# Turning C and a quarter of x on VectorE, and adding 12 readouts by f32 transfers, in a gated mix of a state-space layer and an FFN

## The chip, the core and the metric

One core of one Trainium2 chip runs the kernel. The metric is the device time of one execution in microseconds (us), the median of several runs. One execution of the kernel before was also recorded by the hardware profiler; the profile and its trace come from that one. TensorE (PE), VectorE (DVE), ScalarE (ACT) and GpSimd (POOL) each work through a fixed list of instructions in order; SyncE (SP), ScalarE and GpSimd issue transfers (DMAs), which 16 DMA engines carry out.

## What is computed

x has 2048 tokens of 448 features; everything is bf16 at the borders. Cut to what matters:

```python
dt = exp(log_dt); Lam = Lambda_re + 1j*Lambda_im          # 448 lanes
Lam_bar = exp(dt*Lam)
B_bar = ((Lam_bar - 1)/Lam)[:, None] * (B_re + 1j*B_im)
Bu = x @ B_bar.T                                          # (2048, 448) complex
h[t] = Lam_bar * h[t-1] + Bu[t]                           # recurrence over tokens
a = 2*real(h @ (C_re + 1j*C_im).T) + x*Dskip
b = silu(x @ w1) @ w2                                     # 448 -> 1792 -> 448
g = sigmoid(sum(x*gate_w))                                # per token
out = g*a + (1 - g)*b
```

## The kernel before

**Tiling.** The tokens go in four chunks (tc 0 to 3) of 512, and each chunk in four blocks (tb) of 128. The complex lanes fill seven slots of 128 partitions (NSLOT): slots 0 to 2 the real parts of lanes 0 to 383, slots 4 to 6 their imaginary parts, slot 3 the real and imaginary parts of the last 64 lanes.

**Stages of a chunk.** `x_transposes` turns x on TensorE (32 transposes of 64 by 64 for a chunk, L508) into `xT`, with PSUM copied out by ScalarE or VectorE (L516, L518); chunk 0 has its own (L478). `x_products` (L663) multiplies xT with w1 (F tiles, 14 of 128 columns) and with B (B tiles, 7), two tiles at a time on the two row halves of the array; a pair takes two of eight PSUM banks. `evict` empties them: F tiles through ScalarE's SiLU (L634) into `aT`, B tiles into `UG`, by VectorE for chunk 0 (L640) and by ScalarE for the others (L642). `lanes` does the recurrence on VectorE: products with cosines and sines (L704), seven scans (L736) into `Gf` in f32, a cast of these back into `UG` (by GpSimd's transfers, L390, for chunks 0 to 2; by ScalarE, L746, for chunk 3), and four more products into `H[tc]`. For chunk 0 the first products are 18 small operations (L712 to L725), for the others four large ones. `gates` makes g and 1 - g and puts g*x*Dskip into `Tb` (which is `xnat`). `ffn2` (G in the calls, L774) multiplies aT with w2 per token block; ScalarE scales the result by 1 - g into `fe` (L780), and a GpSimd transfer adds it to Tb (L782). `readout` (C in the calls, L795) multiplies H with the scaled weights `CP`; VectorE multiplies the result by g and adds Tb into `ot` (L798), and SP stores it (L801).

**C.** `load_C` brings C in eight transfers into `Cnat`, which shares the tile H2C with H[2]. `readout_weights(k)` turns a quarter of it on TensorE (16 transposes of 56 by 56, L814), ScalarE scales the two parts into `ct` (L822, L825), and VectorE combines them into CP (L827, L830). The calls cp(0) to cp(3) stand between the G's of chunk 0. CP must be whole before the first readout.

**Order.** TensorE executes in the order of the program. Every other operation carries a cost, a priority and, for transfers, a number of bytes; the planner (`Plan.order`) goes through them with these costs and fixes the order of each engine: what can start first goes first, ties by the lower priority number. A transfer ends in its reckoning at the end of its queue's pipe; SP's and GpSimd's queues have separate pipes:

```python
free[o.eng] = t + o.cost
q = "pool" if o.eng == "pool" else "hw"
pipe[q] = max(pipe.get(q, 0.0), t + 0.9) + o.bytes / self.RATE[q]
o.end = pipe[q] + 0.8
```

The engines then keep that order, with semaphore waits for the true dependencies.

**Order on TensorE (the calls at L867 to L883).** F(0), B(0) and B(1) with the fillers (parameters, B's transposes, x's chunk 1); cp and G(0 to 3); F(1), one F(2), B(2) with x's chunk 2; G(4 to 7); C(0 to 3); F(2), B(3), F(3) with x's chunk 3; C(4 to 7), G(8 to 11); C(8 to 11), G(12 to 15), C(12 to 15).

Of the kernel before, what the change touches and what calls it, by code (L numbers as in the profile page):

```python
# [24 lines left out]
NFILL = 2  # L25
XCOL = [0, 128, 256, 320]
# [250 lines left out]
def bass_gated_mix__ssm_conv_s5__dense_activation_silu__prompt_kernel(nc, A_x, A_Lambda_re, A_Lambda_im, A_B_re, A_B_im, A_C_re, A_C_im,  # L277
               A_log_dt, A_Dskip, B_x, B_w1, B_w2, gate_w, out):
    with ExitStack() as ctx:
# [9 lines left out]
        xT = sb("xT", [128, 4, S_TOK], BF16)  # L289
# [3 lines left out]
        CP = sb("CP", [128, NSLOT, D_MOD], BF16)  # L293
# [5 lines left out]
        H2C = sb("H2C", [128, 3840], BF16)  # L299
        H = [H2C[:, 0:3584].rearrange("p (s n) -> p s n", s=NSLOT) if k == 2 else sb(f"H{k}", [128, NSLOT, CH], BF16) for k in range(4)]  # L300
        Cnat = H2C[:, :].rearrange("p (b l) -> p b l", b=4)
        cnn = [f"H2_{s}" for s in range(7)] + ["H2_3i"]
# [91 lines left out]
        def load_w1(q, k, a, b):  # L394

            cols = slice(w1cuts[k], w1cuts[k + 1])
            src = B_w1[320:448, cols] if a == 3 else B_w1[128 * a:128 * b, cols].rearrange("(b p) f -> p b f", p=128)
            load(q, w1s[:, 3, cols] if a == 3 else w1s[:, a:b, cols], src, " ".join(f"w1_{k}_{i}" for i in range(a, b)),
                 256 * (b - a) * (cols.stop - cols.start))
# [3 lines left out]
        load_w1("sp", 0, 0, 2)  # L403
        load_w1("act", 0, 2, 3)
        load_w1("act", 0, 3, 4)
        for k in range(1, len(w1cuts) - 2):
            load_w1("sp", k, 0, 3)
            load_w1("sp", k, 3, 4)
        for k, v in enumerate((A_log_dt, A_Lambda_re, A_Lambda_im)):
            load("sp", prm[k:k + 1, 0:448], v.rearrange("(o n) -> o n", o=1), f"prm{k}", 896)  # L410
        Bnat = H[3][:, :, 0:D_MOD]
# [5 lines left out]
        load_w1("sp", len(w1cuts) - 2, 0, 3)  # L417
        load_w1("sp", len(w1cuts) - 2, 3, 4)
# [8 lines left out]
        def load_C():  # L427

            for h in range(2):
                rows = lambda a: a[224 * h:224 * h + 224, :].rearrange("(b p) l -> p b l", p=56)  # L430
                to = Cnat[64 * h:64 * h + 56]
                load("sp", to[:, :, 0:448], rows(A_C_re), f"Cn0{h} " + (" ".join(cnn) if h == 0 else ""), 224 * 896)
                load("sp", to[:, :, 576:960], rows(A_C_im[:, 0:384]), f"Cn1{h}", 224 * 768)
                load("sp", to[:, :, 448:512], rows(A_C_im[:, 384:448]), f"Cn2{h}", 224 * 300)
                load("sp", to[:, :, 512:576], rows(A_C_re[:, 384:448]), f"Cn3{h}", 224 * 300)

        load_xn(1)
# [30 lines left out]
        def x0_transposes(q0, part, who):  # L468
# [12 lines left out]
            for h in range(2):  # L481
                src = lambda h=h: bk(tk, h).bitcast(BF16)[:, 0:256].rearrange("p (q b n) -> p q b n", q=2, n=64)
                dst = xT[:, q0:q0 + 2, 256 * part:256 * part + 256].rearrange("p q (b h n) -> p q b h n", h=2, n=64)[:, :, :, h, :]
# [11 lines left out]
        xn_of = {tc: {q: [f"xT{tc}_{h}" for h in range(2)] for q in range(4)} for tc in range(1, NCH)}  # L495
        xn_of[0] = {q: [f"xT0_{q}{part}{h}" for part in range(2) for h in range(2)] for q in range(4)}

        def x_transposes(tc, who):
# [13 lines left out]
            for h in range(2):  # L512
                src = lambda h=h: bk(tk, h).bitcast(BF16).rearrange("p (q b n) -> p q b n", q=4, b=4)
                dst = xT[:, :, tc * CH:(tc + 1) * CH].rearrange("p q (b h n) -> p q b h n", h=2, n=64)[:, :, :, h, :]
                if who[h] == "d":
                    DVE(lambda e, src=src, dst=dst: e.tensor_copy(dst, src()), [tk], [f"xT{tc}_{h}"], 0.69, 2.2, "xTe")  # L516
                else:
                    ACT(lambda e, src=src, dst=dst: e.activation(dst, src(), AF.Copy), [tk], [f"xT{tc}_{h}"], act_cost(1024), 2.2, "xTe")  # L518

# [103 lines left out]
        def evict(pair, tk):  # L623

            kinds = [t[0] for t in pair]
            for k, n in ((0, 2),) if pair[0][:2] == pair[-1][:2] and len(pair) == 2 else ((0, 1), (1, 1))[:len(pair)]:
# [12 lines left out]
                if tc == 0:  # L639
# [7 lines left out]
        def x_products(tiles, fill={}, wait=()):  # L647
# [10 lines left out]
            def steps(k, h, a, z):  # L658
                def body(pe):
                    for n, cut in list(enumerate(part[h]))[a:z]:  # L660
                        for b, ((i, p0), tile) in enumerate(zip(cut, pairs[k])):
                            tc = tile[1]
                            r = pe.matmul(bk(toks[k], b), weights(tile, p0, p0 + 64, i), xT[p0:p0 + 64, i, tc * CH:(tc + 1) * CH],  # L663
# [42 lines left out]
        def lanes(tc):  # L706
# [5 lines left out]
            if tc == 0:  # L712
# [20 lines left out]
            for s in (3, 0, 4, 1, 5, 2, 6) if tc else (0, 4, 1, 5, 2, 6, 3):  # L733
# [52 lines left out]
        def readout(tb):  # L786
# [3 lines left out]
            for n, (a, b) in enumerate(cuts):  # L790
# [6 lines left out]
                PE(mm, [f"H{tc}_{s}" for s in range(7)] + [f"CP{s}" for s in range(NSLOT)], [tk], NSLOT * (0.0025 + (b - a) / 2400), f"C{tc}")  # L797
                DVE(lambda e, tk=tk, a=a, b=b: e.scalar_tensor_tensor(ot[tb % NOT][:, a:b], bk(tk)[:, 0:b - a], g[:, tb:tb + 1],  # L798
# [4 lines left out]

        def readout_weights(k):

            tk = Ps(2)

            def mm(pe):
                for j, c0 in ((0, 128 * k), (1, 448 if k == 3 else 576 + 128 * k)):
                    for b in range(4):  # L810
                        o = j * 224 + 56 * b
                        for h in range(2):
                            p = slice(64 * h, 64 * h + 56)
                            r = pe.transpose(bk(tk, h).bitcast(BF16)[:, o:o + 56], Cnat[p, b, c0:c0 + 128], ident[p, p])  # L814
                return r
            PE(mm, [f"Cn{n}{h}" for n in range(4) for h in range(2)] + cnn + ["ident"], [tk], 8 * 0.0285, "CT")
            both_banks = lambda j: bk2(tk).rearrange("p h n -> p (h n)").bitcast(BF16).rearrange("p (h n) -> p h n", h=2)[:, :, 224 * j:224 * j + 224]
            re = lambda: both_banks(0)
            im = lambda: both_banks(1)
            in_two = lambda a: a.rearrange("p (h n) -> p h n", h=2)  # L820
            c, cn = ct[k % 2], f"ct{k % 2}"
            ACT(lambda e: e.activation(in_two(c[:, 0, :]), im(), AF.Copy, scale=sc2[:, k:k + 1]), [tk, "sc2"], [cn + "a"], act_cost(448, 1), 3, "ct")  # L822
            both = [cn + "a"]
            if k < 3:
                ACT(lambda e: e.activation(in_two(c[:, 1, :]), re(), AF.Copy, scale=sc2[:, k:k + 1]), [tk, "sc2"], [cn + "b"], act_cost(448, 1), 3, "ct")  # L825
                both.append(cn + "b")
            DVE(lambda e: e.scalar_tensor_tensor(in_two(CP[:, k, :]), re(), sc1[:, k:k + 1], in_two(c[:, 0, :]), ALU.mult, ALU.add),  # L827
                [tk, "sc1"] + both, [f"CP{k}"], 0.68, 1, "CP")
            if k < 3:
                DVE(lambda e: e.scalar_tensor_tensor(in_two(CP[:, 4 + k, :]), im(), nsc1[:, k:k + 1], in_two(c[:, 1, :]), ALU.mult, ALU.add),  # L830
                    [tk, "sc1"] + both, [f"CP{4 + k}"], 0.68, 1, "CP")

        def gates(tc):
# [3 lines left out]
               xnn + ["gwb"] + (["Gf0"] if tc else []), ["xg"], 1792, 19, "xg")  # L837
            tt(xnat[:, b4, :], xnat[:, b4, :], dkb[:, None, :].to_broadcast([128, 4, D_MOD]), ALU.mult,
               xnn + ["dkb"] + (["Gf0"] if tc else []), [f"xd{tc}"] + xnn, 1792, 19, "xd")
# [21 lines left out]
        def C(*tbs):  # L861
# [6 lines left out]
                   {(1, 0): [parameters], (K - 2, 0): turn_b[:1], K - 2: turn_b[1:2], K - 1: turn_b[2:], 7: xt(1, "da") + [lambda: lanes(0)]}, [K - 2])  # L868
# [3 lines left out]
        for f in cp(0) + G(0, 1) + cp(1, 2) + G(2, 3) + cp(3):  # L872
            f()
        x_products(F(1) + F(2, 0, 1) + B(2), {2: xt(2, "aa")})
# [44 lines left out]
```

## Time and profile before

| | us |
|---|---|
| median of 3 runs | 141.78 (141.49 to 141.81) |
| the profiled execution | 141.25 |
| its span, first to last instruction | 139.5 |
| VectorE busy, last lane product of chunk 3 ends at | 122.0, 128.16 |
| ScalarE busy | 90.3 |
| GpSimd busy | 39.2 |
| TensorE from the first to the last matmul | 0.76 to 136.73 |
| first readout, last four readouts begin on TensorE | 67.94, 131.38 |
| last transfer issued by SP before the stores, first store | 22.95, 70.3 |

Times in the profile are us from the span's start. The granted TensorE clock was 0.998 of full speed. The page's slices show TensorE busy nine tenths or more in all but the first and the last of 40. The DMA engines are busy through the first 27 us (the loads), and again in bursts, above all where GpSimd's transfers cast the scans (43 to 52, 64 to 76, 89 to 92 us).

### The profile page before, as it was taken

How to read it: one execution, taken by the hardware profiler on the slowest of the kernel's cores; microseconds unless marked ns; L12 is line 12 of the kernel's file. 1: busy time of each engine (PE TensorE's matmuls, PEld its weight loads, DVE VectorE, ACT ScalarE, POOL GpSimd, SP SyncE). 2: the span in 40 equal slices, each digit the busy share in tenths (PEclk: the TensorE clock that was granted, in tenths of full speed). 3: DMA queues.
4: the chain of work that ended last, by engine and by line, in shares of the span. 5: the costliest groups of instructions: out<-in, count | busy, mean ns of one | idle time of the engine just before them, and what ended most of it. 6: DMA issues, size and time to landing. Idle time of an engine off the chain costs nothing.

```text
span 139.5 us, 3000 instructions
## 1 busy us (share of the span) xinstructions
PE 135.9 (97%) x1201; PEld 67.0 (48%) x1201; DVE 122.0 (87%) x179; ACT 90.3 (65%) x157; POOL 39.2 (28%) x72
## 2 busy tenths in 40 slices
PE   7999999999999999999999999999999999999992
PEld 2445454455544544455544544444455555555561
DVE  0319999999999999999999999999999999997053
ACT  3349768999989999823694887799931268312300
POOL 7134040100248440227733001824000314022220
PEclk9999999999999999999999999999999999999999
DMA  4998999510156770104976200674202322323242
GB/s 136 337 294 243 363 320 238 177 42 0 31 79 94 129 110 1 38 15 73 157 131 155 38 5 0 95 133 79 38 4 97 66 33 36 83 83 61 40 94 71
DMA packets 17956, 14.71 MB, mean 105 GB/s; under 512 B 2835, under 2 KB 17814, under 8 KB 17942
## 3 DMA queue, kind: packets, MB, share of 16 engines
q0 software_dynamic: 6064, 5.51, 24.8%
q1 hardware_dynamic: 11318, 8.65, 20.7%
q10 hardware_dynamic: 560, 0.36, 0.8%
q8 instruction: 9, 0.15, 0.4%
q14 instruction: 5, 0.04, 0.1%
HBM read 7.17 MB, written 1.84 MB: 65 GB/s over the span
## 4 chain that ended last, share of the span: by engine, by line
PE 97%; DVE 0%; issue 0%
PE ps L663 46%; PE ps L774 31%; PE ps L795 15%; PE ps L463 2%; PE ps L508 1%; PE ps L478 1%; PE ps L814 1%; PE ps L604 1%; DVE ot L798 0%; PE ps L675 0%; PE ps L464 0%; PE ps L536 0%
## 5 line engine op out<-in xcount | busy, mean ns | idle before, releaser
L663 PE MATMUL ps<-xT,w1s 64*128 64x512 bf16 x392 | 48.5, 378 | 0.0
L774 PE MATMUL ps<-w2s,aT 128*128 128x448 bf16 x224 | 43.2, 353 | 0.0
L634 ACT ACTIVATE aT<-ps 128x1024 bf16<-128x1024 f32 (+1 forms) x30 | 28.7, 969 | 8.5 <-PE ps L663 8.4
L774 PEld LDWEIGHTS ps<-w2s,aT 128*128 128x128 bf16 x224 | 21.7, 98 | 20.4 <-ACT xnat L849 0.4
L663 PEld LDWEIGHTS ps<-xT,w1s 64*128 64x128 bf16 x392 | 19.7, 94 | 22.3 <-DVE xT L486 0.7
L663 PE MATMUL ps<-xT,BT 64*128 64x512 bf16 x196 | 25.8, 376 | 0.0
L782 POOL DMA_DIRECT2D xnat<-fe x16 | 14.1, 900 | 37.9 <-ACT fe L780 37.2
L780 ACT ACTIVATE fe<-ps,g 128x448 bf16<-128x448 f32 x16 | 10.1, 632 | 21.1 <-PE ps L774 21.0
L390 POOL DMA_DIRECT2D UG<-Gf x27 | 14.7, 549 | 20.9 <-DVE Gf L736 20.4
L736 DVE TENSOR_TENSOR_SCAN Gf<-rc,gin,H 128x512 f32<-128x512 f32 x14 | 17.2, 1268 | 0.0
L795 PE MATMUL ps<-CP,H 128*128 128x448 bf16 (+2 forms) x98 | 16.4, 326 | 0.0
L663 PEld LDWEIGHTS ps<-xT,BT 64*128 64x128 bf16 x196 | 10.8, 94 | 11.1 <-DVE Gf L562 0.2
L798 DVE SCALAR_TENSOR_TENSOR ot<-ps,g,xnat 128x448 bf16<-128x448 f32 (+2 forms) x18 | 10.8, 622 | 6.0 <-issue 4.6
L390 POOL DMA_DIRECT2D UG<-UG x8 | 4.8, 597 | 29.2 <-ACT UG L642 17.4
L704 DVE TENSOR_TENSOR H<-UG,COS 128x3584 bf16<-128x3584 bf16 (+4 forms) x10 | 12.6, 1266 | 0.0
L795 PEld LDWEIGHTS ps<-CP,H 128*128 128x128 bf16 x98 | 8.9, 98 | 7.5 <-DVE k L752 0.4
L642 ACT ACTIVATE UG<-ps 128x1024 bf16<-128x1024 f32 (+1 forms) x12 | 10.7, 923 | 1.4 <-PE ps L663 1.4
L842 ACT ACTIVATE junk<-xg 128x448 bf16<-128x448 bf16 x16 | 9.2, 574 | 2.1 <-DVE xg L704 2.0
L849 ACT ACTIVATE xnat<-xnat,g 128x448 bf16<-128x448 bf16 x16 | 9.8, 671 | 0.2
L704 DVE TENSOR_TENSOR PI<-UG,SIN 128x512 bf16<-128x512 bf16 (+2 forms) x13 | 9.1, 722 | 0.0
L704 DVE TENSOR_TENSOR PO<-UG,SIN 128x1536 bf16<-128x1536 bf16 (+1 forms) x8 | 8.7, 1087 | 0.1
L736 DVE TENSOR_TENSOR_SCAN Gf<-rc,gin,H2C 128x512 f32<-128x512 f32 x7 | 8.5, 1265 | 0.0
(102 smaller groups left out, 126.5 us busy)
## 6 DMA issues: line engine op xcount, KB each, us to landing
UG<-Gf POOLq DMA_DIRECT2D x21, 128.0 KB, 2.5
xnat<-fe POOLq DMA_DIRECT2D x16, 112.0 KB, 2.6
out_dram<-ot SPq DMA_DIRECT2D x15, 112.0 KB, 1.7
w2s<-in_B_w_dram SPq DMA_DIRECT2D x1, 1568.0 KB, 11.8
xnat<-in_A_x_dram SPq DMA_DIRECT2D x3, 448.0 KB, 6.1
w1s<-in_B_w_dram SPq DMA_DIRECT2D x1, 576.0 KB, 6.2
UG<-UG POOLq DMA_DIRECT2D x8, 64.0 KB, 2.2
H2C<-in_A_C_re_dram SPq DMA_DIRECT2D x2, 196.0 KB
```

The costliest lines, as they stand in the source:

```text
L390: P.add(q, lambda e: e.dma_start(dst, src), list(after), name.split(), 0.6 if q == "pool" else 0.5, prio, sem(), nbytes, tag="ld " + name)
L634: ACT(lambda e, src=src, dst=dst: e.activation(dst, src(), AF.Silu), [tk, "tbl"], [f"aT{tc % 2}_{m}" for m in names], act_cost(512 * n), 2 ...
L642: ACT(lambda e, src=src, dst=dst: e.activation(dst, src(), AF.Copy), [tk], [f"{un}{m}" for m in names], act_cost(512 * n), 5, "U")
L663: r = pe.matmul(bk(toks[k], b), weights(tile, p0, p0 + 64, i), xT[p0:p0 + 64, i, tc * CH:(tc + 1) * CH], start=(h == 0 and n == 0), stop=( ...
L704: DVE(lambda e: e.tensor_tensor(o, a, b, op), r, w, dve_cost(n, 2), prio, tag)
L736: DVE(lambda e, s=s, b=b, init=init: e.tensor_tensor_scan(Gf[:, s, :], rc[:, b:b + 1].to_broadcast([128, CH]), A[:, s, :], init, ALU.mult, ...
L774: r = pe.matmul(bk(tk)[:, 0:D_MOD], aT[tc % 2][:, fb, o:o + 128], w2s[:, fb, :], start=(fb == 0), stop=(fb == NFB - 1))
L780: ACT(lambda e: e.activation(f[:, :], bk(tk)[:, 0:D_MOD], AF.Copy, scale=g1[:, tb:tb + 1]), [tk, f"g1_{tc}"], [fn], act_cost(448, 1), 7, "fe")
L782: P.add("pool", lambda e: e.dma_start(Tb[:, tb, :], f[:, :], accum_op=ALU.add), [fn, f"Tb{tb}"], [f"Tb{tb}"], 0.94, 2, sem(), 115000, tag= ...
L795: r = pe.matmul(bk(tk)[:, 0:b - a], H[tc][:, s, o:o + 128], CP[:, s, a:b], start=(s == 0), stop=(s == NSLOT - 1))
L798: DVE(lambda e, tk=tk, a=a, b=b: e.scalar_tensor_tensor(ot[tb % NOT][:, a:b], bk(tk)[:, 0:b - a], g[:, tb:tb + 1], Tb[:, tb, a:b], ALU.mul ...
L849: ACT(lambda e, tb=tb: e.activation(Tb[:, tb, :], xnat[:, tb, :], AF.Copy, scale=g[:, tb:tb + 1]), [f"xd{tc}", f"g_{tc}"], [f"Tb{tb}"], ac ...
```

## The change

- **C.** `load_C` brings it in six transfers, rows on 128 partitions, into H[2] (the last block's 64 missing rows are zeroed by GpSimd). `readout_columns` turns it on VectorE in 32 by 32 blocks, four instructions, into H[3], and sixteen SP transfers, one for each pair of 32-partition groups, carry the blocks to their places in CP (runs of 64 bytes). `readout_weights` then scales CP in place. TensorE's transposes of C are gone, and the cp calls come after G(0 to 3).
- **x's chunk 3.** `x_blocks(3)` does the same with x's last 512 tokens: four block turns on VectorE, sixteen transfers into xT. TensorE's transposes and ScalarE's two copies of that chunk are gone.
- **Readouts 0 to 11.** ScalarE scales the PSUM result by g into an f32 tile (`ct`), a GpSimd transfer adds it to Tb, and SP stores Tb. Readouts 12 to 15 stay as they were.
- **Smaller edits.** lanes(0) takes the four large products; gates(1) has priority 20.3 for 19 and CP 20.5 for 1; x's chunk 1 and the parameters' transposes come one step earlier on TensorE; w1 is loaded in pieces of two row blocks each, the second ones of the first two column ranges from ScalarE's queue; the parameter rows are loaded before w1's third range; xT and CP have other layouts.

```diff
+L0M = True
+XT1K = 6
+S0 = (0, 4, 1, 5, 2, 6, 3)
+XT1 = "da"
+XPRIO = {2: 15, 3: 20.5}
+XBLK = (3,)
+XBEH = {2: "PI_0", 3: "H0_0"}
+UDVE = (0, 1, 2, 3, 4, 5, 6)
+OUTA = tuple(range(12))
+PRMF = (0, 0)
+CPRIO = 15.5
+CPP = 20.5
+GPR = (19, 20.3, 19, 19)
+CBEH = "PI_0"
...
-        xT = sb("xT", [128, 4, S_TOK], BF16)
+        xT = sb("xT", [128, NCH, 4, CH], BF16)
-        CP = sb("CP", [128, NSLOT, D_MOD], BF16)
+        CP = sb("CP", [128, NSLOT, CH], BF16)
...
+            if b == 4:
+                src = bass.AP(B_w1.tensor, 128 * a * F_FF + cols.start, [[F_FF, 128], [(320 - 128 * a) * F_FF, 2], [1, n]])
...
+        for k in range(2):
+            load_w1("sp", k, 0, 2)
+            load_w1("act", k, 2, 4)
         for k, v in enumerate((A_log_dt, A_Lambda_re, A_Lambda_im)):
             load("sp", prm[k:k + 1, 0:448], v.rearrange("(o n) -> o n", o=1), f"prm{k}", 896)
+        load_w1("sp", 2, 0, 2)
+        load_w1("sp", 2, 2, 4)
...
+            n = 0
+            for b0, b1, p in ((0, 3, 128), (3, 4, 64)):
+                rows = lambda a: a[128 * b0:128 * b0 + p * (b1 - b0), :].rearrange("(b p) l -> p b l", p=p)
+                for dst, src in (((0, 448), rows(A_C_re)), ((512, 896), rows(A_C_im[:, 0:384])), ((448, 512), rows(A_C_im[:, 384:448]))):
+                    load("sp", Cnat[0:p, b0:b1, dst[0]:dst[1]], src, f"Cn{n}" + (" " + " ".join(cnn) if n == 0 else ""),
+                         p * (b1 - b0) * max(300, 2 * (dst[1] - dst[0])), None, ["Cnz"] * b0)
+                    n += 1
+        POOL(lambda e: e.memset(Cnat[:, 3, :], 0.0), [], ["Cnz"], 0.9, 5)
...
+        def x_blocks(tc):
+            X32 = (xT[:, 3, :, :] if tc == 2 else H[3][:, 0:4, :]).rearrange("p m (q b i) -> p m q b i", q=4, i=32)
+            names = [f"X32_{k}" if tc == 3 else f"XT32_{k}" for k in range(4)]
+            held = [f"H3_{s}" for s in range(7)] + ["H3_3i"] if tc == 3 else xn_of[3][0]
+            turned = [f"BT{s}_{h}" for s in range(7) for h in range(2)]
+            xs = xnat[:, 4 * tc:4 * tc + 4, :]
+            for k, (q0, q1, c, b0, b1) in enumerate(((0, 3, 0, 0, 2), (0, 3, 0, 2, 4), (3, 4, XCOL[3], 0, 2), (3, 4, XCOL[3], 2, 4))):
+                n = q1 - q0
+                src = xs[:, b0:b1, c:c + 128 * n].rearrange("p b (q m i) -> p b q m i", q=n, i=32)
+                dst = X32.rearrange("p m q b i -> p b q m i")[:, b0:b1, q0:q1, :, :]
+                DVE(lambda e, dst=dst, src=src: e.transpose(dst, src), [f"xn{tc}", XBEH[tc]] + turned, [names[k]], 0.15 + 256 * n / 960, XPRIO[tc], "xTd")
+            k = sem()
+            for g in range(4):
+                for m in range(4):
+                    to = xT[32 * m:32 * m + 32, tc, :, :].rearrange("p q (b g i) -> p (q b) g i", b=4, i=32)[:, :, g, :]
+                    P.add("sp", lambda e, to=to, g=g, m=m: e.dma_start(to, X32[32 * g:32 * g + 32, m, :, :, :].rearrange("p q b i -> p (q b) i")),
+                          names + held, [f"xT{tc}_{g}{m}"], 0.66, 400, k, 32768, tag="xTm")
...
-            if tc == 0:
+            if tc == 0 and not L0M:
...
+                if tb in OUTA:
+                    f, fn = ct[tb // 2 % 2][:, tb % 2, :], f"ct{tb // 2 % 2}{'ab'[tb % 2]}"
+                    ACT(lambda e, tk=tk, f=f: e.activation(f, bk(tk)[:, 0:D_MOD], AF.Copy, scale=g[:, tb:tb + 1]),
+                        [tk, f"g_{tc}"], [fn], act_cost(448, 1), 3, "out")
+                    P.add("pool", lambda e, f=f: e.dma_start(Tb[:, tb, :], f, accum_op=ALU.add), [fn, f"Tb{tb}"], [f"Tb{tb}"], 0.94, 2, sem(), 230000, tag="Tb+")
+                    P.add("sp", lambda e: e.dma_start(out2[t0:t0 + 128, :], Tb[:, tb, :]), [f"Tb{tb}"], [], 0.3, 1, outs[tb % NOT], 128 * 896, tag="st")
+                    continue
...
+        def readout_columns():
+            C32 = H[3][:, :, :].rearrange("p s n -> p (s n)").rearrange("p (m t b i) -> p m t b i", m=4, b=4, i=32)
+            names = [f"X32_{k}" for k in range(4)]
...
+            for b in range(4):
+                src = Cnat[:, b, :].rearrange("p (t m i) -> p t m i", m=4, i=32)
+                dst = C32.rearrange("p m t b i -> p b t m i")[:, b, :, :, :]
+                DVE(lambda e, dst=dst, src=src: e.transpose(dst, src), [f"Cn{n}" for n in range(6)] + ["Cnz", CBEH] + cnn + turned, [names[b]],
+                    0.15 + 896 / 960, CPRIO, "CTd")
+            k = sem()
+            for g in range(4):
+                for m in range(4):
+                    to = CP[32 * m:32 * m + 32, :, :].rearrange("p t (b g i) -> p (t b) g i", b=4, i=32)[:, :, g, :]
+                    P.add("sp", lambda e, to=to, g=g, m=m: e.dma_start(to, C32[32 * g:32 * g + 32, m, :, :, :].rearrange("p t b i -> p (t b) i")),
+                          names + held, [f"CT{g}{m}"], 0.66, 400, k, 57344, tag="CTm")
         def readout_weights(k):
-            tk = Ps(2)
-            def mm(pe):
...
-            PE(mm, [f"Cn{n}{h}" for n in range(4) for h in range(2)] + cnn + ["ident"], [tk], 8 * 0.0285, "CT")
...
+            re, im = CP[:, k, 0:D_MOD], CP[:, 4 + k, 0:D_MOD] if k < 3 else None
...
+                ACT(lambda e: e.activation(c[:, 0, :], im, AF.Copy, scale=sc2[:, k:k + 1]), ctn + ["sc2"], [cn + "a"], act_cost(448, 1), 3, "ct")
...
-                   {(1, 0): [parameters], (K - 2, 0): turn_b[:1], K - 2: turn_b[1:2], K - 1: turn_b[2:], 7: xt(1, "da") + [lambda: lanes(0)]}, [K - 2])
+                   {PRMF: [parameters], (K - 2, 0): turn_b[:1], K - 2: turn_b[1:2], K - 1: turn_b[2:], XT1K: xt(1, XT1), 8: [lambda: lanes(0)] + [lambda: x_blocks(2)] * (2 in XBLK) + [readout_columns]}, [K - 2])
...
-        for f in cp(0) + G(0, 1) + cp(1, 2) + G(2, 3) + cp(3):
+        for f in G(0, 1, 2, 3):
+            f()
+        for f in cp(0, 1, 2, 3):
             f()
+        if 3 in XBLK:
+            x_blocks(3)
...
-        x_products(F(2, 1) + B(3) + F(3), {1: xt(3, "aa"), 9: [lambda: gates(3), lambda: lanes(3)]})
+        x_products(F(2, 1) + B(3) + F(3), {1: xt(3, "aa") if 3 not in XBLK else [], 9: [lambda: gates(3), lambda: lanes(3)]})
```

## The prediction

> **What bounds the kernel now.** I read the page's busy line and the chain of waits first, then the timelines of VectorE and ScalarE, then the DMA view in short windows. The profiled execution took 141.25 us, its span is 139.5, and 1.75 lie around it; the median of the runs shown is 141.78. A gain found in the span is taken from that median.
>
> ```profile
> PE 135.9 (97%) x1201; PEld 67.0 (48%) x1201; DVE 122.0 (87%) x179; ACT 90.3 (65%) x157; POOL 39.2 (28%) x72
> PE 97%; DVE 0%; issue 0%
> ```
>
> TensorE carries the chain from 0.76 to 136.73 us. Only what it has to execute, and what makes it wait, moves the time. The chain in order of time (start, length, what) shows what the change touches:
>
> ```profile
> 28.31 0.21 PE ps L814 x16
> ...
> 33.92 0.52 PE ps L814 x32
> ...
> 39.84 0.31 PE ps L814 x16
> ...
> 67.94 5.30 PE ps L795 x28
> ...
> 77.23 0.47 PE ps L508 x32
> ...
> 131.38 5.35 PE ps L795 x42
> ```
>
> L814 turns C and the last L508 turns x's last 512 tokens. Each piece follows its predecessor without a gap. L795 at 67.94 is the first readout, which needs C turned and scaled (CP) and H0; L795 at 131.38 needs H3.
>
> VectorE is the second engine to watch. Its timeline (start, length, what) near the end:
>
> ```profile
> 124.07 2.09 DVE L704 TENSOR_TENSOR H<-UG,COS 128x2048 bf16<-128x2048 bf16 x2
> 126.07 2.09 DVE L704 TENSOR_TENSOR H<-H,PO 128x2048 bf16<-128x2048 bf16 x2
> 132.80 0.69 DVE L798 SCALAR_TENSOR_TENSOR ot<-ps,g,xnat 128x448 bf16<-128x448 f32 x1 [4.64 <-issue]
> ```
>
> From 11 us to 128.16 it shows no idle time, and H3 is ready only 3.2 us before the readout at 131.38 wants it. What is added to VectorE or makes it wait beyond that is paid in full.
>
> **What TensorE loses.** The 64 matmuls of L814 go: 0.21 + 0.52 + 0.31 = 1.04 us. The 32 of L508 for the last 512 tokens go: 0.47. Together 1.51 us of the chain. Nothing is added to TensorE; parameter transposes and x's second chunk only move up by one step. The parameters' rows now have one load of 512 KB fewer ahead of them in SP's queue, 1.5 us at the 340 GB/s of those microseconds, and TensorE asks for them 1.5 us earlier (14 matmuls of 0.108): nothing gained or lost; up to 1.45 lost if they don't land earlier, up to 0.37 (its one wait for w1) won by the joined w1 loads. I take 0.
>
> **VectorE's sum.** By the distance from start to start: 12 readouts of 0.59 leave (7.1). lanes(0)'s 18 products become four of 1.9, 0.9, 1.1 and 1.95 as in lanes(1): 5.9 for 6.85, 1.0 less. Added are four block turns of C (896 columns each) and four of x (two of 768, two of 256). The trace has no such operation. Low end: the bf16 copy BT, 768 columns in 0.47, makes 3.5 us of all; high end: the scan, 512 columns in 1.13, makes 12.4. I take the rate nearest to it, one element per cycle, as the cast of 512 columns in 0.60: C 4 x 1.0, x 2 x 0.87 + 2 x 0.33, together 6.4. CP's seven operations stay. Net -1.7 us (-4.6 to +4.3): VectorE ends at about 126.5, TensorE now asks for H3 at 131.38 - 1.51 = 129.87; slack 3.4 us. At the high end it would be 2.6 late.
>
> **ScalarE, POOL, SP.** ScalarE gets 12 readouts of about 0.55 and one more CP operation of 0.52, and loses two copies of 0.9: +5.3 us on 90.3. Idle time covers it (8.5 us between 58.8 and 67.5, 5.1 before 107.58). POOL gets 12 issues of about 0.86 (L782's row) and a small memset; it idles 100 us. SP issues 32 transfers at some 0.6 (C's and B's loads took 0.54 to 0.88): it idles from 22.95 to 70.3. The f32 sums land some 2.6 us later (row of xnat<-fe) and only a store waits for them.
>
> **The sixteen transfers of C** decide the sign. Each moves 32 partitions x 28 runs of 64 B: 14,336 packets, 896 per DMA engine; x's sixteen make 512 per engine. No row shows 64 B from SBUF to SBUF. Three windows bound a packet. Full rows of 128 B from HBM dominate 22 to 23 us:
>
> ```profile
> DMA packets 409, 0.18 MB, mean 184 GB/s; under 512 B 260, under 2 KB 400, under 8 KB 409
> q1 hardware_dynamic: 389, 0.15, 91.6%
> ```
>
> 0.916 x 16 us over 389 is 37.7 ns. Stores from SBUF, 896 B (135 to 137 us), then 256 B (138.4 to 139.4 us):
>
> ```profile
> q1 hardware_dynamic: 146, 0.12, 16.9%
> ```
>
> ```profile
> q1 hardware_dynamic: 144, 0.03, 15.0%
> ```
>
> 5.41 us over 146 is 37.0 ns; 2.4 over 144 is 16.7. The line through both gives 10.6 ns at 64 B. Low end: bytes alone at w2's 381 GB/s, 2.7 ns. High end: the HBM row, 37.7. I take 10.6, since source and queue are those of the stores: C 9.5 us, x 5.4 us of each engine (2.4 to 33.8 and 1.4 to 19.3).
>
> The Trainium skill ("DMA: Bandwidth & Descriptors", "Why small descriptors are slow (HBM only)") says that transfers within SBUF escape the penalty on short descriptors. If it holds, the stores' line is the right one and not the HBM row; no row here shows it within SBUF.
>
> Now the times. lanes(0) starts at 27.5; its first three products end at 31.4 (C's turn is tied to the third, PI_0), the four turns at 35.4; C had landed by 27.9. The carry then needs 9.5 us beside 5.2 us of POOL's transfers (DMA share times length of the windows from 36 to 46 us: 0.08 x 2, 0.63 x 2, 0.34 x 3, 0.87 x 2, 0.99 x 1) and 1.7 to land (the stores' row): 51.8. Eight ScalarE operations of 0.52 and CP's make it 56; the first readout asks at 66.9. Cover 11 us, gone at 21 ns a packet. x's turn follows H0 and C's carry, its sixteen land by about 73, its products start at 82.07 - 1.51 = 80.6. H0 no longer has CP in front and comes earlier (some 54 for 57.8).
>
> One order is fixed beforehand: the planner charges 0.66 a transfer and has C landed at 35.4 + 15 x 0.66 + 1.9 = 47.2. So ScalarE's ct operations stand where 47.2 is right, and 51.8 makes ScalarE wait 4.6 us there, with SiLU evictions queued behind. Eight PSUM banks are four pairs of 1.51; TensorE goes on for three, 4.5 us, and ScalarE then clears a pair in 0.91. That leaves 0.1 us to pay, and each further microsecond costs one.
>
> **Sum.** 141.25 - 1.51 + 0.1 = 139.84 in the profiled execution, 141.78 - 1.51 + 0.1 = 140.37 in the median: forecast 140.4. Its own range is 139.5 (with the w1 wait and some more) to 141.3.
>
> **Rivals.**
> 1. *ScalarE waits for C's carry (slower).* Place: the first ct operations, F(1)'s evictions behind them, then TensorE without banks. Decides beyond 51.7 us of landing. At 15 ns a packet: 13.4 + 5.5 + 1.7 after 35.4 is 56.0, wait 8.8, less 4.5: 4.3 lost, 140.3 + 4.3 = 144.6. For it: DMA shares of 0.87 to 0.99 from 43 to 47 us and the planner's lack of contention. Against: the 16.7 ns of the stores of 256 B is already near it, with four times the bytes. 0.21.
> 2. *Short packets are no cheaper.* If 64 B cost what the stores' line gives at 512 B (24.9 ns): 22.3 + 6 + 1.7, landing at 65.4, 13.7 us lost: 154. At the HBM row's 37.7 ns some 164. Against: 256 B took less than half of 896 B. 0.07. The Trainium skill ("DMA: Bandwidth & Descriptors", "Specifications") speaks for this one: it puts the least size for line rate at 512 B, below which the engine reads, modifies and writes. By that the result would be the 154 of this rival; the trace's falling price from 896 to 256 B does not agree.
> 3. *Block turns at the scan's rate.* H3 2.6 late: 140.3 + 2.6 = 142.9. 0.06.
> 4. *Given back.* ct (4.2 us) now falls between 39 and 56 us, where ScalarE already has SiLU 6.9, x's copies 1.85, U's 3.3, fe 1.2: 17.45 for 17.0 us; the gates' 5.1 ahead of U's would hold four pairs of banks when FFN's second half asks for one: 1 to 2 us, 141.3 to 142.3. 0.10.
>
> **How the numbers follow.** Forecast 0.56, the rivals 0.21, 0.07, 0.06 and 0.10. 0.3% (0.4 us) is about what tells a change from none. Faster: the forecast's 0.56. Same: rival 4, 0.10. Slower: rivals 1 to 3, 0.34. The range reaches from 139.5 to 145.0, which holds the forecast, rivals 3 and 4 and most of rival 1; what lies beyond is rival 2, the worse part of rival 1 and little below.
>
> **What would show it.** Right: no L814, two L508 groups; C's sixteen landing near 52 us with a packet near 10 ns; block turns of about 1.0 and 0.9 us; chain still TensorE at 97%; H3 before 129.9. Wrong: ScalarE or VectorE idle near 48 us behind the CT transfers, gaps in TensorE after 50 us, SP issues of well over 0.7 us each, or a last readout that waits for VectorE.

## The result and the profile after

The changed kernel takes 153.03 us in the median of six runs (150.71 to 154.08), the kernel before 141.87 in the same comparison (141.49 to 142.43). The ratio is 1.0675, 95% interval 1.0589 to 1.0760: slower, where faster was forecast. The ratio is taken from the runs in the fast state alone (150.71, 150.80 and 152.93 us for the changed kernel), so it lies below the ratio of the two medians; the profiled execution is one of the longer runs. The profiled execution of the changed kernel took 153.14 us, its span is 151.3 (before 139.5): 11.8 us have to be found.

The page of the changed kernel: busy times, the granted TensorE clock in 40 slices, and the shares of the chain by engine.

```profile
span 151.3 us, 2853 instructions
...
PE 138.6 (92%) x1105; PEld 67.7 (45%) x1105; DVE 120.9 (80%) x161; ACT 95.5 (63%) x168; POOL 50.0 (33%) x85
...
PEclk9999999999999995699999999869999999999999
...
PE 52%; DVE 17%; SPq 13%; DMA 10%; issue 4%; ACT 2%; POOL 0%; DVEq 0%; ACTq 0%
```

TensorE, 97% of the chain before, now has about half of it; SP's queue and the DMAs have 23%. TensorE has 96 instructions less, as intended, and yet is busy 2.7 us longer: the clock row shows two dips (5, 6 and 8, 6 tenths), and each matmul takes longer there. The timeline of TensorE in the changed kernel (start, length, what; in brackets the idle time before it and what ended it) has these gaps after the first microseconds:

```profile
8.55 2.55 PE L701 MATMUL ps<-xT,w1s 64*128 64x512 bf16 x22 [0.69 <-DMA w1s<-in_B_w_dram]
...
58.15 6.35 PE L701 MATMUL ps<-xT,BT 64*128 64x512 bf16 x34 [5.13 <-ACT aT L672]
...
97.59 1.89 PE L701 MATMUL ps<-xT,w1s 64*128 64x512 bf16 x8 [2.53 <-ACT UG L680]
```

The stretch that follows each of the two large gaps is itself slow: 34 matmuls in 6.35 us, where 0.108 each makes 3.67. Windows of the same trace (length, busy time of PE, PEld, DVE, ACT and POOL with counts, granted clock, DMA share, GB/s) show the clock go down to half after the first gap and stay there for nearly 7 us, from about 56.4 to 63.3:

```profile
54.00:56.00 2.00, 0.00 (x0) 0.00 (x0) 2.00 (x2) 0.00 (x0) 0.00 (x0) 1.00 0.71 85
56.00:58.00 2.00, 0.00 (x0) 0.00 (x0) 0.29 (x1) 1.48 (x3) 0.00 (x0) 0.61 0.02 2
58.00:60.00 2.00, 1.85 (x10) 0.73 (x12) 1.24 (x2) 2.00 (x4) 0.00 (x0) 0.50 0.00 0
60.00:62.00 2.00, 2.00 (x14) 0.63 (x10) 2.00 (x3) 2.00 (x5) 0.06 (x1) 0.50 0.00 0
62.00:64.00 2.00, 2.00 (x16) 0.81 (x14) 2.00 (x4) 1.22 (x4) 0.99 (x2) 0.69 0.27 66
```

The account of TensorE up to the last four readouts, which begin at 142.44 for 131.38 before: +0.47 in the first 28 us, where TensorE waits for w1, +5.13 and +2.68 (6.35 - 3.67) for the first gap and its slow stretch, +2.53 for the second gap and +1.58 for its stretch (97.59 to 110.49 takes 12.90 us, the same 104 matmuls before 11.32), -1.51 for the transposes that are gone. Together +10.88 of 11.06; some 0.2 is unassigned, and 0.7 more lies behind the last matmuls.

What stands behind the gaps is in the view of waits of the changed kernel (who waits for what: us in total, times, longest):

```profile
DVE PO L742 <- DMA UG<-Gf: 7.7, 3, 3.3
...
ACT ct L875 <- DMA CP<-H: 6.8, 1, 6.8
...
PE ps L701 <- ACT aT L672: 5.1, 1, 5.1
ACT UG L680 <- DVE H L742: 4.3, 1, 4.3
...
PE ps L701 <- ACT UG L680: 2.5, 1, 2.5
```

The first gap is one chain: TensorE lacks banks because ScalarE's SiLU (aT) doesn't run; ScalarE stands 6.8 us before its first `ct` because C's sixteen transfers (CP<-H) have not landed. ScalarE's timeline around it:

```profile
47.77 1.96 ACT L672 ACTIVATE aT<-ps 128x1024 bf16<-128x1024 f32 x2
56.52 0.67 ACT L875 ACTIVATE ct<-CP,scc 128x448 f32<-128x448 bf16 x1 [6.79 <-DMA CP<-H]
57.09 1.00 ACT L672 ACTIVATE aT<-ps 128x1024 bf16<-128x1024 f32 x1
```

The second gap is another: VectorE's products of lanes(1) wait for casts (UG<-Gf), lanes(1) ends late, ScalarE may not yet overwrite UG[1] with U of chunk 3, and TensorE stops. VectorE's timeline there:

```profile
91.73 0.96 DVE L742 TENSOR_TENSOR PO<-UG,SIN 128x1536 bf16<-128x1536 bf16 x1 [3.35 <-DMA UG<-Gf]
93.68 1.23 DVE L742 TENSOR_TENSOR PO<-UG,SIN 128x2048 bf16<-128x2048 bf16 x1 [0.98 <-DMA UG<-Gf]
```

VectorE also came late to lanes(1): before it, it had waited 3.3 us for the casts of lanes(0) and 4.3 us in all for `ct`. H3, the one that the prediction watched on VectorE, is ready at 137.97 for a readout at 142.44.

Why C lands at 56.5: the chain of waits of the changed kernel in order of time, with the time that each transfer's issue held SP's queue,

```profile
36.45 0.73 SPq L866
...
43.38 1.60 SPq L866
...
48.83 2.92 SPq L866
...
53.45 0.66 SPq L866
54.15 2.34 DMA CP<-H
```

and the DMA view of the changed kernel, queue by queue (packets, MB, share of 16 engines), from 44 to 48 us and from 52 to 56 us:

```profile
q0 software_dynamic: 554, 0.50, 82.6%
q1 hardware_dynamic: 1901, 0.12, 32.9%
```

```profile
q1 hardware_dynamic: 5092, 0.32, 71.8%
q0 software_dynamic: 29, 0.02, 3.2%
```

q0 is GpSimd's queue (the casts of lanes(0)), q1 SP's. While the casts have the engines, C moves 1901 packets in 4 us; alone it moves 5092. The shares of the two queues add up to 115% from 44 to 48 us, so some packet times overlap. An issue on SP takes 0.66 us behind the casts, at 53.45, and up to 2.92 beside them.

### The profile page after: what moved, and what is told of

It is laid out like the page before. It is cut to its first block, busy times and chain, and to the rows that moved or that the text cites. A ratio compares the mean times of both kernels' runs of the same rounds, so it can differ in the third digit from the quotient of the medians.

```text
span 151.3 us, 2853 instructions
## 1 busy us (share of the span) xinstructions
PE 138.6 (92%) x1105; PEld 67.7 (45%) x1105; DVE 120.9 (80%) x161; ACT 95.5 (63%) x168; POOL 50.0 (33%) x85
## 4 chain that ended last, share of the span: by engine, by line
PE 52%; DVE 17%; SPq 13%; DMA 10%; issue 4%; ACT 2%; POOL 0%; DVEq 0%; ACTq 0%
PE ps L812 21%; PE ps L701 17%; PE ps L833 13%; SPq L866 11%; DMA UG<-Gf 5%; DMA w1s<-in_B_w_dram 3%; DVE H L860 3%; DVE UG L678 3%; SPq L403 2%; DVE Gf L565 2%; DMA CP<-H 2%; DVE H L742 1%; ACT aT L672 1%; DVE PI L742 1%; DVE ot L843 1%
## 5 line engine op out<-in xcount | busy, mean ns | idle before, releaser
L701 PE MATMUL ps<-xT,BT 64*128 64x512 bf16 x196 | 29.2, 415 | 5.1 <-ACT aT L672 5.1
L701 PEld LDWEIGHTS ps<-xT,w1s 64*128 64x128 bf16 x392 | 20.3, 95 | 26.4 <-issue 3.2
L774 DVE TENSOR_TENSOR_SCAN Gf<-rc,gin,H 128x512 f32<-128x512 f32 x21 | 25.4, 1267 | 0.1
L403 POOL DMA_DIRECT2D UG<-Gf x27 | 18.3, 776 | 11.8 <-DVE Gf L774 11.4
L833 PE MATMUL ps<-CP,H 128*128 128x448 bf16 (+2 forms) x126 | 21.9, 332 | 0.0
L701 PEld LDWEIGHTS ps<-xT,BT 64*128 64x128 bf16 x196 | 12.1, 102 | 18.3 <-ACT aT L672 5.9
L742 DVE TENSOR_TENSOR H<-UG,COS 128x3584 bf16<-128x3584 bf16 (+2 forms) x9 | 16.2, 1809 | 0.0
L833 PEld LDWEIGHTS ps<-CP,H 128*128 128x128 bf16 x126 | 11.6, 98 | 10.0 <-issue 0.4
L680 ACT ACTIVATE UG<-ps 128x1024 bf16<-128x1024 f32 (+1 forms) x12 | 10.6, 917 | 6.5 <-DVE H L742 4.3
L840 POOL DMA_DIRECT2D xnat<-ct x12 | 12.2, 1152 | 4.3 <-ACT ct L838 2.7
L843 DVE SCALAR_TENSOR_TENSOR ot<-ps,g,xnat 128x448 bf16<-128x448 f32 (+2 forms) x6 | 3.0, 525 | 7.2 <-PE ps L833 7.2
L742 DVE TENSOR_TENSOR PI<-UG,SIN 128x1536 bf16<-128x1536 bf16 (+1 forms) x8 | 8.5, 1078 | 0.0
```

What stands on the lines that cost most here:

```text
L403: P.add(q, lambda e: e.dma_start(dst, src), list(after), name.split(), 0.6 if q == "pool" else 0.5, prio, sem(), nbytes, tag="ld " + name)
L742: DVE(lambda e: e.tensor_tensor(o, a, b, op), r, w, dve_cost(n, 2), prio, tag)
L774: DVE(lambda e, s=s, b=b, init=init: e.tensor_tensor_scan(Gf[:, s, :], rc[:, b:b + 1].to_broadcast([128, CH]), A[:, s, :], init, ALU.mult, ...
L833: r = pe.matmul(bk(tk)[:, 0:b - a], H[tc][:, s, o:o + 128], CP[:, s, a:b], start=(s == 0), stop=(s == NSLOT - 1))
L840: P.add("pool", lambda e, f=f: e.dma_start(Tb[:, tb, :], f, accum_op=ALU.add), [fn, f"Tb{tb}"], [f"Tb{tb}"], 0.94, 2, sem(), 230000, tag=" ...
```

## Experiments

Times in brackets are the range of the runs; the kernel before took 141.5 to 141.9 in these comparisons.

**C reckoned late.** The planner reckoned that C lands at 47.8 (the prediction had estimated 47.2). Here it is told more bytes, so that it expects C at 58.5 and puts ScalarE's ct there.

```diff
-  names + held, [f"CT{g}{m}"], 0.66, 400, k, 57344, tag="CTm")
+  names + held, [f"CT{g}{m}"], 0.66, 400, k, 390000, tag="CTm")
```

> The planner is told that the sixteen transfers of C take as long as they did (landing near 58 us in its reckoning, for 47.8), so ct and CP stand later in ScalarE's and VectorE's order; nothing else changes. Theory A (ScalarE waits at ct for C's carry, and SiLU evictions queue behind it): ScalarE's 6.8 us of idle time before ct and TensorE's 5.1 us gap at 53 us go, and the half clock after it; C still lands near 56 us. VectorE's lanes(1) stays late, so the second gap (97 us) stays or grows: 143 to 148 us. Rival B (the f32 readouts through GpSimd's queue cost the time): no change, 151 to 153 us. Rival C (VectorE simply has too much to do before lanes(1), whoever waits): the first gap goes but all of it comes back in the second, 150 to 153 us.

Measured 153.93 us (153.22 to 154.96), ratio 1.0872 [1.0816, 1.0928]. The first gap and ScalarE's 6.8 us of idle time are gone, so the chain C, ct, SiLU, banks is shown. But the time came back at once, though not at the second gap, where rival C had it. TensorE's waits in this kernel:

```profile
PE ps L701 <- DMA xT<-H: 7.6, 1, 7.6
PE ps L833 <- DVE CP L881: 2.8, 1, 2.8
```

CP is now ready after the first readout wants it, and x's sixteen transfers, in turn behind it and among lanes(1)'s casts, run from 70.2 to 91 us and arrive 7.6 us late. There was no room to wait for C where it was; and the second carry has the same fault as the first.

**C turned early.** The four turns of C are no longer tied to a product of lanes(0); they run as soon as C has landed.

```diff
-CBEH = "PI_0"
+CBEH = "Cnz"
```

> C's block turns no longer wait for the third product of lanes(0); they go as soon as C has landed, so the carry runs before lanes(0)'s casts instead of beside them. Theory A: C lands near 41 us with SP issuing one transfer in 0.66 us, no wait at ct, no wait of VectorE for the casts near 48 us; lanes(1)'s scans start near 69 us for 75; first gap gone, second at most 2 us: 141 to 144 us. Rival D (64-byte packets are the cost wherever they run): C lands 18 us after its first issue again and little is gained, 149 us or more. Rival C: 147 us or more.

Measured 150.97 us (150.31 to 152.02), ratio 1.0664 [1.0603, 1.0726]. The issues go from 28.95 to 41.4 and the last lands at 45.4, eleven us earlier, though not near 41 as expected: the sixteen issues alone hold SP for 12.5 us, most of them before the casts fill the engines, and the last packets meet the casts. And the planner now reckons with 40.0 and puts ct accordingly: ScalarE still waits 5.8 us for CP<-H, TensorE 3.9 for ScalarE. Starting earlier moves the expected time with it. What makes ScalarE wait is the difference between the landing and the one reckoned with: 5.4 us here and a wait of 5.8, 8.7 us in the changed kernel and a wait of 6.8.

**No f32 readouts.** All readouts by VectorE again.

```diff
-OUTA = tuple(range(12))
+OUTA = ()
```

> All 16 readouts go through VectorE as before; no f32 sums through GpSimd's queue. Theory A: first gap unchanged (C's carry is untouched); VectorE has 7 us more to do, 2.4 of them before lanes(1) is through: second gap the same or up to 3 us more, 151 to 156 us. Rival B (the f32 transfers stand in front of lanes(1)'s casts and fill the DMA engines): second gap gone, 146 to 149 us.

Measured 151.75 us (151.25 to 151.95), ratio 1.0701 [1.0658, 1.0743]. The first gap stays (5.4). The second shrinks from 2.5 to 0.4 us, and VectorE no longer waits for lanes(1)'s casts, so the f32 transfers among them had a part in it; in exchange VectorE is late at the end, and the last readouts wait 1.9 us for H3. No net gain.

**x's chunk 3 by TensorE.** The second carry is taken away.

```diff
-XBLK = (3,)
+XBLK = ()
```

> x's last 512 tokens are turned by TensorE again; C stays with VectorE. Theory A: first gap unchanged at 5 us; lanes(1) comes 2.5 us earlier for the missing block turns and its casts have no transfers of x beside them, so the second gap goes: 146 to 149 us, of which 0.5 us is TensorE's own transposes. Rival B: no change in the second gap, 151 to 154 us.

Measured 149.18 us (148.04 to 149.43), ratio 1.0515 [1.0464, 1.0566]. The first gap is unchanged at 5.0, the second gone, and VectorE's wait for lanes(1)'s casts has shrunk from 4.3 to 0.2 us. Either of these two runs takes away, or nearly so, the second gap: it needs both x's part of the change and the f32 transfers. That both stand in the way of lanes(1)'s casts fits the waits; this run also takes x's block turns, 2.7 us, off VectorE, and does not tell the two apart.

**Both carries early and reckoned as they are.** The turns of C and of x run as soon as their source is there (x's priority raised), and the planner is given bytes that make each carry as long as it was seen to be.

```diff
-CBEH = "PI_0"; XBEH = {2: "PI_0", 3: "H0_0"}; XPRIO = {2: 15, 3: 20.5}
+CBEH = "Cnz";  XBEH = {2: "PI_0", 3: "Cnz"};  XPRIO = {2: 15, 3: 15}
-  [f"CT{g}{m}"], 0.66, 400, k, 57344       [f"xT{tc}_{g}{m}"], 0.66, 400, k, 32768
+  [f"CT{g}{m}"], 0.66, 400, k, 290000      [f"xT{tc}_{g}{m}"], 0.66, 400, k, 230000
```

> Both carries out of the casts' way and out of the fixed order's error: C is turned as soon as it has landed, the planner reckons its landing near 45 us (as measured in the run with C turned early), and x's last tokens are turned right behind it (priority 15, no wait for H0), while VectorE waited for casts before; their carry is reckoned to end near 62 us. Theory A (DMA engines shared between carries and casts, in an order fixed for less): no gap of TensorE above 1 us after 10 us, lanes(1)'s scans start near 66 us, H3 before the last readouts; 140.5 to 143 us. Rival C (VectorE has too much before lanes(1)): the gap near 95 us stays at 2 us or more and the time at 145 us or more.

Measured 143.06 us (142.13 to 145.71), ratio 1.0096 [1.0060, 1.0132]. Of the 6.75 points above the kernel before, 5.8 are gone with every instruction of the change still there. The place of the carries and the reckoning cost them, not the work; the run changes both at once and does not say what each is worth. C's issues go from 28.81 to 42.3, x's from 49.32 to 60.8. One gap above 1 us is left, where none was expected. What TensorE still waits for after 8 us: 0.73 for w1 and

```profile
89.53 1.04 PE L701 MATMUL ps<-xT,w1s 64*128 64x512 bf16 x8 [2.06 <-ACT UG L680]
```

**w1's loads as before.** The kernel above, with w1's second column range on SP's queue again, the parameter rows behind the third, and the parameters' transposes one step later on TensorE.

```diff
-PRMF = (0, 0)
+PRMF = (1, 0)
...
-for k in range(2):
-    load_w1("sp", k, 0, 2); load_w1("act", k, 2, 4)
+load_w1("sp", 0, 0, 2); load_w1("act", 0, 2, 4)
+for k in (1, 2):
+    load_w1("sp", k, 0, 2); load_w1("sp", k, 2, 4)
...
-load_w1("sp", 2, 0, 2); load_w1("sp", 2, 2, 4)
```

> As the run before, with w1's third range again ahead of the parameter rows, its second range on SP alone and the parameters' transposes one step later, as in the kernel before. Theory E (w1's third range lands 0.7 us after TensorE wants it): TensorE's wait for w1 at 7.9 us goes, 0.5 us less than the run with both early. Rival: no difference beyond 0.2 us, as another wait takes its place.

Measured 142.86 us (142.63 to 143.56), ratio 1.0091 [1.0061, 1.0121]: no gain that can be told. The wait for w1 is gone, and 0.84 us of waiting for ScalarE (UG) came up at 56.98. A wait of 0.7 us near 8 us was not what bounded the rest.

**C loaded before w2.** The kernel above with `load_C()` ahead of w2's load. VectorE no longer waits for C.

> As the run with w1 back, with C loaded ahead of w2, so that VectorE doesn't wait for C (0.9 us in the run with C turned early) before its block turns. Theory A: C's carry starts where VectorE's order has it, some 28.5 us; within 0.5 us of the run with w1 back, 0 to 0.9 us better if VectorE's end decides. If w2 becomes late for the FFN's second half at 28 us, 1 us worse.

Measured 142.19 us (141.30 to 143.67), ratio 1.0029 [0.9997, 1.0062]: not to be told from the kernel before. One gap of 1.21 us is left, at 87.79, for UG of ScalarE behind lanes(1).

**C alone.** The kernel of 142.86 us (w1 as before, C early) with x's chunk 3 by TensorE.

```diff
-XBLK = (3,)
+XBLK = ()
```

> C turned early by VectorE and carried, with the honest reckoning; x's last tokens by TensorE, w1 as before, readouts 0 to 11 still by ScalarE and f32 transfers. Theory A: no second carry at all, lanes(1) some 2.5 us earlier than with x's block turns; TensorE saves 1.04 us only: 140.7 to 142 us. Rival B (f32 transfers cost): 143 us or more.

Measured 143.02 us (142.72 to 143.56), ratio 1.0107 [1.0071, 1.0143]. It was expected at 140.7 to 142. Three small waits of TensorE for ScalarE's SiLU, 0.25 to 0.59 us each, have taken the place of the one near 89. The time is the one that the rival gave, by which the f32 transfers cost it; the runs with fewer of them, below, are no faster. Against the same kernel with x's turn (142.86) there is no difference: rightly placed, x's turn neither wins nor costs anything that can be told.

**Four sevenths of C's bytes.** The changed kernel itself, each transfer of C with 16 runs of 64 B a partition for 28, the number of issues and the order the same. The last three slots of CP are set to zero by GpSimd (its line is left out here), so the outputs leave out part of the state.

```diff
-  to = CP[32 * m:32 * m + 32, :, :].rearrange("p t (b g i) -> p (t b) g i", b=4, i=32)[:, :, g, :]
+  to = CP[32 * m:32 * m + 32, :, :].rearrange("p t (b g i) -> p (t b) g i", b=4, i=32)[:, 0:16, g, :]
-  C32[32 * g:32 * g + 32, m, :, :, :].rearrange("p t b i -> p (t b) i")
+  C32[32 * g:32 * g + 32, m, 0:4, :, :].rearrange("p t b i -> p (t b) i")
```

> The changed kernel with four of seven slots carried: each of the sixteen transfers of C moves 16 runs of 64 B a partition and not 28; the last three slots of CP stay at zero (a POOL memset near 5 us), so the outputs leave out part of the state. Number of issues, their place and the planned order are unchanged. Theory A (the carry is late because the bytes of packets share the DMA engines with the casts of lanes(0), C's share 8.9 us of each engine): 3.8 us of it go, C lands near 52, ScalarE's wait for it falls from 6.8 to about 3, TensorE's gap from 5.1 to 1 to 1.7, the stretch at half clock behind it shortens or goes: 147 to 149.5. Rival B (the number of issues on SP, 16 of them at up to 2.9 us, or the casts alone set it): the gap stays at 5, 152 to 154.

Measured 147.42 us (146.81 to 148.37), ratio 1.0409 [1.0368, 1.0450]. Waits of this kernel (its lines are one higher):

```profile
ACT ct L876 <- DMA CP<-H: 3.3, 1, 3.3
```

```profile
PE ps L702 <- ACT UG L681: 3.8, 1, 3.8
PE ps L702 <- ACT aT L673: 1.7, 1, 1.7
```

ScalarE's wait falls by 3.5 us and the gap by 3.4, for 3.8 us of packets taken out (three sevenths of 8.9): here the packets decide, not the number of issues. The 34 matmuls behind the gap take 3.84 us now for 6.35; a gap of 1.7 us cost no clock. The second gap has grown to 3.8 us, and VectorE waits 4.2 us for lanes(1)'s casts as before.

**Fewer f32 readouts in the good order.** The kernel of 142.19 us with readouts 0 to 3 by VectorE, so that no f32 transfer stands among lanes(1)'s casts (the f32 readouts' stores get semaphores of their own); and the same with none at all.

```diff
-OUTA = tuple(range(12))
+OUTA = tuple(range(4, 12))
```

> The kernel with both turns early, w1 back and C loaded first (142.19), with readouts 0 to 3 by VectorE again and 4 to 11 through f32 transfers. Theory A (the last gap of 1.21 us in TensorE, U's eviction behind lanes(1), comes from four f32 transfers of readouts that stand among lanes(1)'s casts on POOL's queue between 69 and 77 us): the gap goes, VectorE gets 2.4 us more early where it waits anyhow, 140.4 to 141.4. Rival (it was x's carry and the casts' own length): gap stays near 1, 142 to 142.6.

> As the run before, with none of the readouts through f32 transfers (all by VectorE). VectorE then has 7.1 us more work than in 142.19. Theory A: the gap near 88 us goes as well, but lanes(3) ends late as it did when the same was done to the changed kernel (its readout waited 1.9 us there): 141 to 143. Rival (VectorE's relief by 12 readouts isn't needed once the turns are early, since the 6.4 us of turns now lie in idle time): under 141.

Measured 142.55 us (141.86 to 144.45), ratio 1.0055 [1.0034, 1.0076], and 144.36 (144.15 to 145.06), ratio 1.0193 [1.0166, 1.0219]. With readouts 0 to 3 by VectorE no cast is waited for, and the gap has not gone but grown:

```profile
88.66 1.04 PE L701 MATMUL ps<-xT,w1s 64*128 64x512 bf16 x8 [1.73 <-ACT UG L680]
```

VectorE shows no idle time from 11 to 95 us in this kernel. So the expectation fell, and what is left as the cause of the last gap is VectorE's own lateness. Its block turns come before lanes(1), and the readouts that leave it begin only at 68 us. With none of the f32 readouts the last readouts wait 1.9 us for H3 besides: the relief is needed at the end.

**The gates of chunk 2 later.** The kernel of 142.19 us; two VectorE products of 1.07 us go behind lanes(1)'s scans.

```diff
-GPR = (19, 20.3, 19, 19)
+GPR = (19, 20.3, 22, 19)
```

> The kernel of 142.19 us with the gates of the third chunk (two VectorE products of 1.07 us, at 71.8 and 74.0) behind lanes(1)'s scans and not between them. Theory C (what is left of the loss is the order on VectorE: the block turns come before lanes(1), the relief by f32 readouts only after it, so lanes(1) ends 1.2 us after TensorE needs UG[1] read; the run with readouts 0 to 3 on VectorE showed a gap of 1.73 us with no wait for a cast): lanes(1)'s scans end 2.1 us earlier, the gap near 88 us goes, median 140.8 to 141.4, under before's 141.6. Rival (the casts of lanes(1) between f32 transfers on POOL's queue set it): the wait of 1.4 us for a cast grows to 3 and the gap stays at 1: 142 to 142.5.

Measured 141.18 us (140.28 to 142.77), beside 141.90 (141.29 to 143.97) of the kernel before on the same chip: ratio 0.9953 [0.9923, 0.9982]. TensorE's waits in this kernel, all of 0.2 us and more:

```profile
PE ps L479 <- PEq L962: 0.8, 1, 0.8
PE ps L833 <- ACT aT L672: 0.2, 1, 0.2
```

The first of them is there in every run. The gap is gone, though VectorE's one wait for a cast grew from 1.4 to 2.4 us: the order on VectorE had set it. The last four readouts begin at 130.01, 1.37 us earlier than in the kernel before, nearly all of the 1.51 that the transposes were worth; the profiled execution took 140.28 us, its span is 138.5. This version holds the three main parts of the change, with w1's loads nearly as before; it is faster than the kernel before by about a half per cent.

## Why the prediction was wrong, point by point

**What TensorE loses: right.** The transposes are gone, 1.51 us. "I take 0" for w1 and the parameters was 0.47 off, inside the bounds it gave, though it was w1's third range that came late and not the parameter rows.

**VectorE's sum: right as a sum, blind to its order.** A block turn of C takes 1.0 us as predicted, those of x 0.97 and 0.44 for 0.87 and 0.33:

```profile
32.34 4.08 DVE L860 STREAM_TRANSPOSE H<-H 128x896 bf16<-128x896 bf16 x4
...
51.19 0.96 DVE L742 TENSOR_TENSOR PO<-UG,SIN 128x1536 bf16<-128x1536 bf16 x1 [3.34 <-DMA UG<-Gf]
...
58.76 0.69 DVE L881 SCALAR_TENSOR_TENSOR CP<-CP,sc1s,ct 128x448 bf16<-128x448 bf16 x1 [2.47 <-ACT ct L876]
```

Busy time went from 122.0 to 120.9 (net -1.1 for -1.7), and H3 has 4.5 us of slack. But the step checked VectorE at one place, the end. The turns are added before lanes(1), the relief comes after 68 us, and lanes(1) has a use of its own: UG[1] must be read before U of chunk 3 may be written. Even with everything else mended that cost 1.2 to 1.7 us at 88 us, until two products were put later.

**The sixteen transfers of C: the price right, the company wrong.** A 64-byte packet alone takes 0.718 x 64 us / 5092 = 9.0 ns, and 9.8 over the whole carry (10.6 taken). The step that failed is the "5.2 us of POOL's transfers" beside it. They were summed over 36 to 46 us, while the landing that this gave was at 51.8: the window ended before the carry did. The trace of before had the rest; its GpSimd queue from 44 to 48 us and from 48 to 52 us:

```profile
q0 software_dynamic: 661, 0.60, 92.8%
```

```profile
q0 software_dynamic: 502, 0.43, 74.6%
```

With the windows from 36 to 44 (35.5% and 43.6%) and the 1.1% after 52 that is 4 x (0.355 + 0.436 + 0.928 + 0.746 + 0.011) = 9.9 us, and 35.4 + 9.5 + 9.9 + 1.7 = 56.5, the time at which ScalarE got C. The changed kernel's own trace has much the same: the turns end at 36.45, and from there to 56.5 us C's packets hold 44.6% of the engines' time and the casts 47.9%, 8.9 and 9.6 us. The experiment with four sevenths of the bytes bears the sum out.

**The cover: the path right, the size by luck.** By the prediction's own rule a landing at 56.5 gives a wait of 9.3, less 4.5 of banks: 4.8 lost. TensorE lost 5.13, but both terms were too large. ScalarE waited 6.8 us, since the work that it had before ct lasted to 49.7; TensorE went on for 3.3 us of that, to 53.0, and began again 1.6 us after C was there: 6.8 - 3.3 + 1.6 = 5.1. So rival 1, ScalarE waiting for C's carry, is what happened, and three of the signs that were named for going wrong came: ScalarE idle from 49.7, a gap in TensorE after 50, issues on SP of up to 2.92 us. Its chance, 0.21, was too low because of the short window; its price, 144.6, left out what a gap brings after it. That was 2.7 us of half clock behind the first gap, and a second gap (2.5 and 1.6 of half clock) from the carry of x and the f32 transfers.

**x's turn, costed at nothing.** "Its sixteen land by about 73": they were issued from 69.42 to 80.3 us, and delayed lanes(1)'s casts (landing 4.4 us in the median for 2.5 before). The prediction counted the casts against C's carry but not against x's. The run with x on TensorE shows the price in this order: the second gap is gone and the ratio falls from 1.0675 to 1.0515.

**The other rivals.** Rival 2's time, 154, is near the result by chance alone: its packets of 24.9 ns were 9.0. A packet got cheaper as it got shorter, which is what the prediction held against this rival, but a byte did not: 37.0, 16.7 and 9.0 ns make 0.041, 0.065 and 0.14 ns a byte at 896, 256 and 64 B. The Trainium skill ("DMA: Bandwidth & Descriptors", "Specifications") puts the least size for line rate at 512 B. The prediction held the falling price per packet against that; the rising price per byte does not refute it. The Trainium skill's section "Why small descriptors are slow (HBM only)" ("DMA: Bandwidth & Descriptors") exempts transfers within SBUF from the penalty on short descriptors. At 9.0 ns for 64 B, over three times the 2.7 ns of the prediction's low end, no full exemption shows here. Rival 3 fell with block turns of 1.0 us. Rival 4, ScalarE too full between 39 and 56 us, did not come to be tested, since ScalarE stood idle there.

## What to carry to other kernels

A transfer's landing time is found by closing the loop: sum what shares the DMA engines up to the landing itself, not up to the first guess. Where a planner fixes the order, an engine waits for a late transfer by about its landing less the landing reckoned with, so give the transfer room to land and correct its reckoning before judging the change, and do so for every transfer of that kind at once: for C alone, either step left the time at 151 to 154 us. Work moved to an engine is checked at each place where something waits for that engine, in the order of time; equal sums hide load that comes early and relief that comes late.

## What the runs showed of the hardware

A packet of 64 bytes within SBUF takes 9.0 ns of an engine's time. The 37.7 ns that the prediction read from HBM at 22 to 23 us is no price of 128-byte rows alone: the 389 packets there carried 0.15 MB, 390 bytes each on average. In the company of casts the 64-byte packet takes 0.329 x 64 us / 1901 = 11.1 ns, and the casts' packets 95 ns from 44 to 48 us, for 90 in the kernel before: beside the casts C's packets are a quarter dearer, and the casts' own hardly.

The issue of such a transfer holds SP for 0.66 us where no cast runs, and up to 2.92 us where casts run, so the next issue is late too.

The clock: TensorE's granted clock fell to 0.50 behind gaps of 2.04 us (C turned early), 2.53 and 5.13 us (the changed kernel) and all longer ones. It stayed at 1.00 behind gaps of 2.06 us (both carries early) and 2.80 us (C reckoned late), and behind all shorter ones. So the length of a gap does not decide it alone:

```profile
94.00:96.00 2.00, 1.19 (x12) 0.60 (x14) 2.00 (x3) 1.84 (x3) 0.96 (x2) 1.00 0.00 0
96.00:98.00 2.00, 2.00 (x14) 0.76 (x10) 2.00 (x2) 1.61 (x2) 0.13 (x1) 0.52 0.29 66
```

```profile
70.00:71.00 1.00, 1.00 (x6) 0.50 (x6) 1.00 (x2) 0.00 (x0) 0.79 (x1) 1.00 0.77 115
```

The first two lines are C turned early, where TensorE began again at 94.81; the third is C reckoned late, where it began again at 69.90. The price varies too: with the slow stretch behind them, gaps of 5.01, 5.13 and 5.43 us cost 6.5, 7.8 and 8.5 us. The Trainium skill ("TensorE: Matmul & The Clock Gate", Part 1 on the HAM clock gate) says that an idle window of some 3.4 us halves the clock and a busy one of that length restores it. The rows agree with the halving; they show it already behind a gap of 2.04 us, and for nearly 7 us behind the one of 5.13.
